# Hash-bit rows of pairs hashed alone, and the place of loads and output weights, in a fused attention and feed-forward kernel

## The chip, the cores and the metric

The kernel runs on one core of one Trainium2 chip. A core has a matrix engine (TensorE, PE in the profile), a vector engine (VectorE, DVE), an activation engine (ScalarE, ACT), a general engine (GpSimd, POOL) and SyncE (SP), which here only issues transfers. Each engine takes its own instructions in the order in which they were written, and waits on semaphores for what other engines and transfers have done. 16 DMA engines carry the transfers. The metric is the device time of one execution in microseconds; the median of several is compared.

## The reference, cut to what matters

Attention over 4 batches, 8 heads, 768 tokens and 64 dimensions. Six random projections give each token a bucket; a query sees only the keys of its own bucket. Behind it stands a gated feed-forward layer over all 3072 tokens.

```python
q_bits = np.einsum('bhsd,dk->bhsk', q, proj) > 0      # 6 bits; k_bits likewise
mask   = q_bucket[:, :, :, None] == k_bucket[:, :, None, :]
scores = np.where(mask, q @ k.T / sqrt(64), -1e9)
attn   = exp(scores - max) / (sum + 1e-9)
x      = (attn @ v) as 3072 x 512
xn     = x / sqrt(mean(x * x) + 1e-6) * rms_g
out    = (silu(xn @ w_gate) * (xn @ w_val)) @ w_out    # 512 -> 1536 -> 512
```

## The kernel before

**The mask is part of the product.** A head's q and k lie transposed in a tile `QK`, rows 0 to 63 the dimensions, rows 64 to 75 twelve rows made from the hash bits. For k a bit gives -32 or 0 and for q 16 or 0, in two rows for each bit, so that a key with another bit lowers the score so far that its exponential vanishes. One matmul over 76 rows (`KROWS`) gives the masked scores (`scores`, L344).

**The unit of work is a pair of heads**, written (batch, pair), as in (1,2). For a pair, q, k and v are loaded (`load_blocks`, L122, in four transfers of 96 KB for q or k with runs of 32 numbers; `load_rows`, L112, for v and for batch 0), turned (`turn_dve`, L194, VectorE, four steps each for k and q; `turn_pe` for batch 0 and pair (1,0)), cast into `QK` (`cast_pool`, L202, GpSimd), hashed, and v is cast and summed by GpSimd (`v_prep` L310, `v_sum` L316 to L318). The loads share ten buffers in turn.

**Hashing**: four products of the projection with k and q into one bank (`hash_bank`, L210), VectorE's comparison, which gives a tile of bits (`signs`, L217), and then the rows are moved to partitions 64 and up of `QK`. The pairs (1,1), (1,2) and (1,3) are hashed alone (`hash_lone`): one bank holds, for each half of the tokens, 32 rows for k and 32 for q, in which 12 rows are of the first head and the next 12 of the second. Eight transfers on SyncE's queue (L285) move 12 rows by 384 each. Pair (1,0) takes eight transfers of L268; batches 2 and 3 are hashed by two pairs at once (`hash_pairs`, L303).

**The order is written out by hand.** The loop runs over 192 slots of attention (a slot is a third of a head of one query half) and 48 more for what trails. `plan[s]` holds what is issued at slot s beside the scores and the exponential (`probs`, L354); `at(s, f, ...)` puts a step there, `rank` orders the steps within a slot. Nothing is moved by a scheduler: a step at a later slot stands behind all earlier steps in its engine's queue. Each transfer on SyncE's queue also waits for the eighth one before it. From slot 42 on, the feed-forward layer of query half w runs beside the attention of the halves after it, over 24 slots for each w: `gate` (L446), `value` (L456) with VectorE's L457 and L458 between, then `project` (L469), which needs the output weights `wo`, `ft` 0 to 5 from the first half's transfer and 6 to 11 from the second's. The hash products and the feed-forward products take turns in three banks of one pool (`gps`).

**Weights** come on GpSimd's own queue, cast on the way (`load_w` L520, `load_wo` L526): `wg` and `wv` in halves at slots 2, 6, 12 and 21, the two halves of `wo` at 43 and 50.

For a pair of `work`, `in_row(loads, s, hash_slot)` gives the slots of the k, q and v loads, the first slot of the eight turning steps, and the slot of the hash; the casts come at s + 4 and s + 8, v at s + 9. The first scores of (1,0) belong to slot 48, those of (1,1) to 60, of (1,2) to 66, of (1,3) to 72.

Of the kernel before, what the change touches and what calls it, by code (L numbers as in the profile page):

```python
# [8 lines left out]
FP32 = mybir.dt.float32  # L9
# [7 lines left out]
S = 768  # L17
D = 64
# [3 lines left out]
HALF = 384  # L22
KROWS = D + 12
# [17 lines left out]
BY_PE = [(0, hp) for hp in range(4)] + [(1, 0)]  # L41
# [3 lines left out]
def kernel(  # L45
# [12 lines left out]
    nc = tc.nc  # L58
    PSUM = bass.MemoryType.PSUM

    const = ctx.enter_context(tc.tile_pool(name="const", bufs=1))
# [20 lines left out]
    thr = const.tile([128, 1], FP32, name="thr")  # L82
    scl = const.tile([128, 1], FP32, name="scl")
    mhalf = const.tile([128, 3], FP32, name="mhalf")
    gcol = const.tile([128, 4], FP32, name="gcol")
    wg = const.tile([128, 4, DFF], FP16, name="wg")
    wv = const.tile([128, 4, DFF], FP16, name="wv")
# [39 lines left out]
    T0, QK = {}, {}  # L127
# [10 lines left out]
    def t0(b, h, which):  # L138
        hp, hh = divmod(h, 2)
        return T0[b, hp, which][:, hh * HALF : (hh + 1) * HALF]  # L140

    def k_cols(b, h, jt):
        o = (jt // 3) * S + (jt % 3) * 128 if (b, h // 2) in BY_PE else S + jt * 128
        return QK[b, h // 2][0:KROWS, h % 2, o : o + 128]

    def q_cols(w, h):
        b, half = divmod(w, 2)
        t = QK[b, h // 2][0:KROWS, h % 2]
        if (b, h // 2) in BY_PE:
            return t[:, half * S + HALF : (half + 1) * S]  # L150
        if b == 1:
            return t[:, 0:S].rearrange("p (c e t) -> p e c t", e=2, t=128)[:, half]
        return t[:, half * HALF : (half + 1) * HALF]
# [53 lines left out]
    def hash_bank(parts):  # L207
        ps = bank("d_ps", [128, HALF])
        for t, (w, src) in enumerate(parts):
            nc.tensor.matmul(  # L210
                ps[32 * t : 32 * t + 32, :], w, src,
                start=True, stop=True, tile_position=(0, 32 * t),
            )
        return ps

    def signs(bt, ps):
        nc.vector.tensor_scalar(  # L217
            out=bt, in0=ps, scalar1=thr, scalar2=scl, op0=ALU.is_gt, op1=ALU.mult
        )
# [6 lines left out]
    def bits_tile(i):  # L226

        if i % 2 == 0:
            held.append(spool.tile([128, S], FP16, name="bits", bufs=3))
        return held[-1][:, (i % 2) * HALF : (i % 2 + 1) * HALF]  # L230
# [43 lines left out]
    def hash_lone(b, hp):  # L274

        ps = hash_bank(
            [(w[:, 0:32], T0[b, hp, which][:, half * HALF : (half + 1) * HALF])
             for half in range(2) for w, which in ((pk, "k"), (pq, "q"))]
        )
        bt = bits_tile(0)  # L280
        signs(bt, ps)
        for hh in range(2):
            for half, j in ((0, 0), (0, 1), (1, 1), (1, 0)):
                p0, o = 64 * half + 32 * j + 12 * hh, (S, 0)[j] + half * HALF
                nc.sync.dma_start(  # L285
                    out=QK[b, hp][D:KROWS, hh, o : o + HALF], in_=bt[p0 : p0 + 12]
                )

    def hash_pairs(b, hps):
# [49 lines left out]
    def scores(g):  # L339
        w, h, p = SLOTS[g]  # L340
        ps = scps.tile([128, 2, 512], FP32, name="s_ps")
        idle(ps[:, 0, HALF:512], {0: 8, 3: 6}.get(g, 0))
        for j in range(2):
            nc.tensor.matmul(  # L344
                ps[:, j, 0:HALF], k_cols(w // 2, h, 2 * p + j), q_cols(w, h),
                start=True, stop=True,
            )
        sps[g] = ps
# [227 lines left out]
    def at(s, f, *a, rank=3):  # L576
        plan[s].append((rank, len(plan[s]), lambda: f(*a)))
# [36 lines left out]
    for i, (t, src) in enumerate(((wg, moe_w_gate), (wv, moe_w_val))):  # L614
        at(2 + 4 * i, load_w, t, src, 0, 768)
        at(12 + 9 * i, load_w, t, src, 768, 1536)
        at(43 + 7 * i, load_wo, 6 * i, 6 * i + 6)


    for which, sl in zip("kqv", (9, 11, 15)):  # L620
        at(sl, load_rows, nc.sync, 1, 0, which)
# [11 lines left out]
    def in_row(loads, s, hash_slot=None):  # L633
        return loads, range(s, s + 8), (s + 4, s + 8, s + 9), hash_slot

    work = {
        (1, 1): in_row((21, 32, 33), 42, 51), (1, 2): in_row((38, 42, 44), 49, 58),
        (1, 3): in_row((46, 52, 54), 56, 65),
        (2, 0): in_row((56, 60, 62), 64), (2, 1): in_row((63, 66, 69), 72, 81),
        (2, 2): in_row((71, 75, 78), 81), (2, 3): in_row((80, 83, 86), 89, 98),  # L640
        (3, 0): in_row((90, 94, 98), 100), (3, 1): in_row((100, 104, 108), 110, 119),
        (3, 2): in_row((116, 120, 124), 126), (3, 3): in_row((126, 130, 134), 136, 145),
    }
    for (b, hp), (loads, turns, cast_slots, sh) in work.items():
        for which, s in zip("kqv", loads):
            at(s, load_rows if which == "v" else load_blocks, nc.sync, b, hp, which)
        for i, s in enumerate(turns):
            at(s, turn_dve, b, hp, "kq"[i // 4], i % 4, rank=5)
        for which, s in zip("kq", cast_slots):
            at(s, cast_pool, b, hp, which)  # L650
        if sh:
            if b == 1:
                at(sh, hash_lone, b, hp)
            else:
                at(sh, hash_pairs, b, (hp - 1, hp))
        at(cast_slots[2], v_prep, b, hp)
        at(cast_slots[2], v_sum, b, hp)
        if b > 1 and hp % 2:
            at(48 * b + (17 if hp == 3 else -4), v_mean, b, hp - 1, 4)
# [18 lines left out]
    for w in range(8):  # L678
# [21 lines left out]
        for i in range(9 if w < 7 else 6):  # L700
            c, j = divmod(i, 3)
# [62 lines left out]
```

## Time and profile before

| | |
|---|---|
| median of 3 runs | 341.2 us (340.05 to 343.66) |
| profiled execution | 340.95 us, its span 339.2 us |
| mean granted clock of TensorE | 0.995 |
| busy in the span | PE 96%, DVE 70%, ACT 61%, POOL 46% |
| SyncE's transfers, share of the 16 DMA engines | 33.4%, in 82000 packets |
| weights on GpSimd's queue, share | 8.8%, in 3712 packets |
| transfers of bits by `hash_lone` | 24, issued from 69.1 to 104.0 us |

A page of the profile tells one execution. A row of a timeline gives the start, the length, the engine, the line, the operation and its operands; in square brackets stands how long the engine was idle before, and what ended that. A row of waits gives who waited for whom, with the total, the number of times and the longest. A window gives the busy time of each engine in a stretch, the clock that TensorE was granted as a share of full speed, the mean busy share of the DMA engines and what they moved. The ends of matmuls are modelled, so neighbours overlap a little. SPq and POOLq are the queues that issue transfers; their rows tell the issue, not the landing.

### The profile page before, as it was taken

Reading aid. Unit: us, or ns where it says so; the run is one execution under the profiler, and the core shown is the slowest. Engines: PE = TensorE matmul, PEld = TensorE weight load, DVE = VectorE, ACT = ScalarE, POOL = GpSimd, SP = SyncE. Lnnn points to the kernel's source line nnn. Section 1 sums busy time; section 2 is a strip of 40 time slices with the busy share of each in tenths; the row PEclk is TensorE's granted clock in tenths of the full one; section 3 lists DMA queues with packets and bytes.
Section 4 is the critical chain, followed back from the end, with each engine's and each line's share of the span. In section 5 each row is a group of like instructions: output and inputs, shape, how many; then the busy total and the mean of one; then the engine's idle time right before and its main releaser. Section 6 shows DMA issues by size and latency. Waiting matters only on the chain.

```text
span 339.2 us, 7797 instructions
## 1 busy us (share of the span) xinstructions
PE 326.1 (96%) x2983; PEld 200.2 (59%) x2983; DVE 237.7 (70%) x532; ACT 207.9 (61%) x324; POOL 155.6 (46%) x230
## 2 busy tenths in 40 slices
PE   8999989599989999999999999999999999999995
PEld 7566666265555655656565655656566655655653
DVE  4789669489587986978767794977356754784860
ACT  3789987356465755666665766666666766532321
POOL 4888766178745586374826156463101311130000
PEclk9999999989999999999999999999999999999999
DMA  7998929947273947605531572000110001001002
GB/s 236 334 231 192 140 50 183 175 79 135 44 177 78 199 56 178 109 9 119 124 82 24 109 121 90 22 12 7 38 56 2 3 31 64 2 1 62 33 0 93
DMA packets 85972, 31.36 MB, mean 92 GB/s; under 512 B 71480, under 2 KB 82992, under 8 KB 85936
## 3 DMA queue, kind: packets, MB, share of 16 engines
q1 hardware_dynamic: 82000, 26.09, 33.4%
q0 software_dynamic: 3712, 4.72, 8.8%
q8 instruction: 23, 0.38, 0.5%
q14 instruction: 13, 0.11, 0.1%
q10 hardware_dynamic: 224, 0.07, 0.1%
HBM read 28.32 MB, written 6.29 MB: 102 GB/s over the span
## 4 chain that ended last, share of the span: by engine, by line
PE 80%; DVE 8%; POOL 3%; DMA 3%; SPq 2%; issue 2%; ACT 1%; DVEq 0%; ACTq 0%; POOLq 0%
PE y_ps L469 18%; PE v_ps L456 16%; PE s_ps L344 14%; PE g_ps L446 13%; PE o_ps L366 8%; PE d_ps L210 4%; PE s_ps L446 3%; DMA kL<-in_k_dram 2%; PE x_ps L431 1%; SPq L122 1%; SPq L285 1%; PE z_ps L337 1%; PE t_ps L170 1%; DMA QK<-bits 1%; DVE t L457 1%
## 5 line engine op out<-in xcount | busy, mean ns | idle before, releaser
L354 ACT ACTIVATE psb<-s_ps 128x768 f16<-128x768 f32 x192 | 150.6, 809 | 33.5 <-PE s_ps L344 31.7
L344 PE MATMUL s_ps<-QK 76*128 76x384 f16 x384 | 93.7, 326 | 3.0 <-DMA QK<-bits 1.3
L456 PE MATMUL v_ps<-xnT,wv 128*128 128x384 f16 x384 | 78.7, 327 | 0.0
L469 PE MATMUL y_ps<-wo,ht 128*128 128x512 f16 x276 | 69.2, 379 | 0.1
L448 ACT ACTIVATE t<-g_ps 128x384 f32<-128x384 f32 x78 | 38.2, 490 | 48.0 <-PE g_ps L446 47.5
L457 DVE SCALAR_TENSOR_TENSOR t<-t,g_ps 128x384 f32<-128x384 f32 x78 | 42.7, 547 | 32.5 <-ACT t L448 32.1
L366 PEld LDWEIGHTS <-psb 128*128 128x128 f16 x1152 | 52.4, 98 | 22.0 <-issue 3.9
L446 PE MATMUL g_ps<-xnT,wg 128*128 128x384 f16 x312 | 63.5, 325 | 1.2 <-DVE xnT L432 0.6
L390 POOL TENSOR_TENSOR x<-otmp,rcp 128x384 f32<-128x384 f32 x31 | 25.9, 835 | 83.6 <-DVE rcp L386 83.1
L458 DVE SCALAR_TENSOR_TENSOR ht<-t,v_ps 128x384 f16<-128x384 f32 x96 | 53.2, 554 | 10.8 <-PE v_ps L456 1.5
L366 PE MATMUL o_ps<-vl,psb 128*128 128x65 f16 x1152 | 56.9, 194 | 0.0
L446 PEld LDWEIGHTS <-wg 128*128 128x128 f16 x384 | 36.1, 97 | 25.2 <-issue 1.7
L456 PEld LDWEIGHTS <-wv 128*128 128x128 f16 x384 | 36.4, 98 | 23.8 <-issue 0.9
L344 PEld LDWEIGHTS <-QK 76*128 76x128 f16 x384 | 31.3, 98 | 20.8 <-issue 8.2
L469 PEld LDWEIGHTS <-ht 128*128 128x128 f16 x276 | 25.9, 97 | 25.1 <-issue 1.5
L476 ACT COPY ysb<-y_ps 128x512 f32<-128x512 f32 x23 | 13.5, 586 | 25.3 <-PE y_ps L469 24.9
L402 POOL TENSOR_TENSOR sq<-x 128x384 f32<-128x384 f32 x31 | 25.7, 827 | 2.5
L432 DVE TENSOR_TENSOR xnT<-x_ps,gcol 128x512 f16<-128x512 f16 x24 | 16.2, 681 | 14.5 <-PE x_ps L431 14.5
L202 POOL CAST QK<-qT 64x768 f16<-64x768 f32 x22 | 18.2, 827 | 17.2 <-DVE qT L194 16.5
L194 DVE STREAM_TRANSPOSE kT<-kL 128x192 f32<-128x192 f32 x44 | 22.1, 516 | 4.3 <-issue 4.3
L381 DVE TENSOR_TENSOR otmp<-o_ps,cvb 128x390 f32<-128x390 f32 x32 | 17.9, 558 | 8.1 <-PE o_ps L366 8.0
L202 POOL CAST QK<-kT 64x768 f16<-64x768 f32 x22 | 18.2, 828 | 10.5 <-PE v_ps L456 4.1
(80 smaller groups left out, 301.7 us busy)
## 6 DMA issues: line engine op xcount, KB each, us to landing
vL<-in_v_dram SPq DMA_DIRECT2D x16, 384.0 KB
out_dram<-ysb SPq DMA_DIRECT2D x23, 256.0 KB
kL<-in_k_dram SPq DMA_DIRECT2D x44, 96.0 KB
qL<-in_q_dram SPq DMA_DIRECT2D x44, 96.0 KB
kL<-in_k_dram SPq DMA_DIRECT2D x4, 384.0 KB
qL<-in_q_dram SPq DMA_DIRECT2D x4, 384.0 KB
wg<-in_moe_w_gate_dram POOLq DMA_DIRECT2D x2, 768.0 KB, 7.2
wv<-in_moe_w_val_dram POOLq DMA_DIRECT2D x2, 768.0 KB, 8.4
```

The costliest lines, as they stand in the source:

```text
L202: nc.gpsimd.tensor_copy(QK[b, hp][0:64, hh, o : o + S], T0[b, hp, which][64 * hh : 64 * hh + 64, :])
L344: nc.tensor.matmul(ps[:, j, 0:HALF], k_cols(w // 2, h, 2 * p + j), q_cols(w, h), start=True, stop=True,)
L354: nc.scalar.activation(psb[w, h][:, p], sps.pop(g)[:, :, 0:HALF], AF.Exp, scale=ESCALE,)
L366: nc.tensor.matmul(o[:, c, hh, 0:65], psb[w, h][:, jt // 2, jt % 2, 128 * c : 128 * c + 128], vls[b % 2][:, h, v_chunk(b, h, jt), 0:65], s ...
L390: eng.tensor_mul(xd.rearrange("p c (h d) -> p c h d", h=2), tmp[:, :, :, 0:64], r.to_broadcast([128, 3, 2, 64]),)
L402: nc.gpsimd.tensor_mul(sq, xd, xd)
L446: nc.tensor.matmul(g, wg[:, kt, fs], xnT[w][:, kt], start=(kt == 0), stop=(kt == 3))
L448: nc.scalar.activation(t, g, AF.Tanh, scale=0.5)
L456: nc.tensor.matmul(vv, wv[:, kt, fs], xnT[w][:, kt], start=(kt == 0), stop=(kt == 3))
L457: nc.vector.scalar_tensor_tensor(out=t, in0=t, scalar=1.0, in1=g, op0=ALU.add, op1=ALU.mult)
L458: nc.vector.scalar_tensor_tensor(out=ht[w][:, ft], in0=t, scalar=0.5, in1=vv, op0=ALU.mult, op1=ALU.mult)
L469: nc.tensor.matmul(y, ht[w][:, ft, c * 128 : (c + 1) * 128], wo[:, ft, :], start=(ft == 0), stop=(ft == NF - 1),)
```

## The change

For pairs hashed alone `QK` keeps 24 rows of bits, and the scores' product runs over 88 rows. k's 24 rows (both heads' twelve) go to both heads' halves of the tile by one transfer for each half of the tokens, whose source is read twice: two transfers on SyncE's queue for a pair. q's 24 rows are written by GpSimd, multiplied row by row by a column of `own`, which is 1 on the rows of the head in question and 0 on the other's; four products of 24 by 384 for a pair. The zero rows of q take the other head's bits of k out of the sum. `own` is set at slot 45 by seven memsets.

The k, q and v loads of (1,1), (1,2) and (1,3) move to earlier slots, those of batch 2 by 2 to 4 slots. The halves of the output weights move from slots 43 and 50 to 31 and 52.

```diff
@@
+    own = const.tile([128, 2], FP32, name="own")
@@
+    def rows_of(b, hp):
+
+        return D + 24 if b == 1 and (b, hp) not in BY_PE else KROWS
+
     def k_cols(b, h, jt):
         o = (jt // 3) * S + (jt % 3) * 128 if (b, h // 2) in BY_PE else S + jt * 128
-        return QK[b, h // 2][0:KROWS, h % 2, o : o + 128]
+        return QK[b, h // 2][0 : rows_of(b, h // 2), h % 2, o : o + 128]
 
     def q_cols(w, h):
         b, half = divmod(w, 2)
-        t = QK[b, h // 2][0:KROWS, h % 2]
+        t = QK[b, h // 2][0 : rows_of(b, h // 2), h % 2]
@@
         bt = bits_tile(0)
         signs(bt, ps)
-        for hh in range(2):
-            for half, j in ((0, 0), (0, 1), (1, 1), (1, 0)):
-                p0, o = 64 * half + 32 * j + 12 * hh, (S, 0)[j] + half * HALF
-                nc.sync.dma_start(
-                    out=QK[b, hp][D:KROWS, hh, o : o + HALF], in_=bt[p0 : p0 + 12]
+        for half in range(2):
+            kb, qb = 64 * half, 64 * half + 32
+            nc.sync.dma_start(
+                out=QK[b, hp][D : D + 24, :, S + half * HALF : S + (half + 1) * HALF],
+                in_=bt[kb : kb + 24].unsqueeze(1).to_broadcast([24, 2, HALF]),
+            )
+            for hh in range(2):
+                nc.gpsimd.tensor_scalar_mul(
+                    QK[b, hp][D : D + 24, hh, half * HALF : (half + 1) * HALF],
+                    bt[qb : qb + 24], own[qb : qb + 24, hh : hh + 1],
                 )
@@
-        at(43 + 7 * i, load_wo, 6 * i, 6 * i + 6)
-
+        at(31 + 21 * i, load_wo, 6 * i, 6 * i + 6)
+
+    def rows_of_heads():
+
+        nc.gpsimd.memset(own, 0.0)
+        for p0 in (32, 96):
+            nc.gpsimd.memset(own[p0 : p0 + 24, 1:2], 1.0)
+            nc.gpsimd.memset(own[p0 : p0 + 12, 1:2], 0.0)
+            nc.gpsimd.memset(own[p0 : p0 + 12, 0:1], 1.0)
+
+    at(45, rows_of_heads)
@@
-        (1, 1): in_row((21, 32, 33), 42, 51), (1, 2): in_row((38, 42, 44), 49, 58),
-        (1, 3): in_row((46, 52, 54), 56, 65),
-        (2, 0): in_row((56, 60, 62), 64), (2, 1): in_row((63, 66, 69), 72, 81),
-        (2, 2): in_row((71, 75, 78), 81), (2, 3): in_row((80, 83, 86), 89, 98),
+        (1, 1): in_row((21, 22, 32), 42, 51), (1, 2): in_row((32, 33, 37), 49, 58),
+        (1, 3): in_row((38, 40, 44), 56, 65),
+        (2, 0): in_row((53, 55, 58), 64), (2, 1): in_row((59, 62, 66), 72, 81),
+        (2, 2): in_row((68, 71, 75), 81), (2, 3): in_row((78, 82, 86), 89, 98),
```

## The prediction

> **What bounds the kernel now.** First the page's head, then TensorE's own waits.
>
> ```profile
> span 339.2 us, 7797 instructions
> PE 326.1 (96%) x2983; PEld 200.2 (59%) x2983; DVE 237.7 (70%) x532; ACT 207.9 (61%) x324; POOL 155.6 (46%) x230
> ```
>
> TensorE (PE) is busy for 96% of the span; all its idle time is 13.1 us. An edit that leaves its matmuls alone can win only from that, and from stretches at a lower clock. Who ends its waits, as total, times and longest in us:
>
> ```profile
> PE d_ps L210 <- DVE t L457: 3.5, 1, 3.5
> PE s_ps L344 <- DMA QK<-bits: 1.3, 2, 1.1
> ```
>
> So two places matter: one wait for VectorE (DVE) at a hash product, two for bits that come by DMA. TensorE's timeline places them, with the products I use below:
>
> ```profile
> 55.87 0.49 PE L344 MATMUL s_ps<-QK 76*128 76x384 f16 x2
> 62.44 0.81 PE L446 MATMUL g_ps<-xnT,wg 128*128 128x384 f16 x4
> 66.73 0.56 PE L210 MATMUL d_ps<-kT,pk 128*32 128x384 f32 x1 [3.48 <-DVE t L457]
> 70.30 0.89 PE L446 MATMUL g_ps<-xnT,wg 128*128 128x384 f16 x4
> 80.40 0.49 PE L344 MATMUL s_ps<-QK 76*128 76x384 f16 x2
> 80.72 1.03 PE L469 MATMUL y_ps<-wo,ht 128*128 128x512 f16 x4
> 102.23 0.49 PE L344 MATMUL s_ps<-QK 76*128 76x384 f16 x2 [1.07 <-DMA QK<-bits]
> 106.77 0.48 PE L344 MATMUL s_ps<-QK 76*128 76x384 f16 x2 [0.23 <-DMA QK<-bits]
> ```
>
> The product at 66.73 is pair (1,1)'s hash (slot 51). The first wait costs more than its length, as the windows show (span, busy time of PE, PEld, DVE, ACT, POOL; then granted clock, DMA share, GB/s):
>
> ```profile
> 66.00:68.00 2.00, 1.27 (x9) 0.26 (x10) 1.86 (x6) 0.00 (x0) 0.00 (x0) 0.76 0.83 194
> 68.00:70.00 2.00, 2.00 (x10) 0.98 (x10) 1.69 (x5) 0.81 (x1) 1.74 (x3) 0.50 1.18 211
> 70.00:72.00 2.00, 2.00 (x19) 1.31 (x17) 1.24 (x3) 0.77 (x2) 1.92 (x3) 0.88 0.37 57
> 102.00:104.00 2.00, 1.77 (x19) 1.20 (x20) 0.84 (x3) 0.60 (x2) 1.11 (x2) 1.00 0.10 21
> ```
>
> After the 3.48 us gap the granted clock falls; the loss is 2 x (0.24 + 0.50 + 0.12) = 1.72 us. After the 1.07 us gap it stays 1.00.
>
> Behind the 3.48 us stands a load. The chain of waits (start, length, what):
>
> ```profile
> 55.60 5.84 DMA kL<-in_k_dram
> 61.44 4.33 issue
> ```
>
> VectorE's next instruction is the transpose of pair (1,2)'s k (slot 49). It has nothing else to wait for, and starts at 61.44 + 4.33 = 65.77; everything on VectorE queues behind it, the pass that frees the bank of the hash product too. Why the load is late, by SyncE's queue (SPq):
>
> ```profile
> 40.68 6.17 SPq L268 DMA_DIRECT2D QK<-bits  x8
> 50.45 8.08 SPq L122 DMA_DIRECT2D kL<-in_k_dram  x4
> 98.56 7.09 SPq L285 DMA_DIRECT2D QK<-bits  x8
> ```
>
> And by packets, MB and share of the DMA engines, from 61 to 62 us and then from 65 to 66 (q0 carries the weights, q1 SyncE's transfers):
>
> ```profile
> q0 software_dynamic: 165, 0.17, 104.3%
> q1 hardware_dynamic: 167, 0.02, 26.6%
> ```
>
> ```profile
> q1 hardware_dynamic: 1401, 0.18, 116.3%
> ```
>
> While output weights are moving, the 128-byte packets of the k loads get one turn for each weight packet, 167 in a microsecond; alone they get 1401. (1,2)'s k loads were issued from 50.45 on, into both halves of the output weights.
>
> **The change, part by part.** *Loads forward, output weights from slot 43 to 31.* q of (1,1) now stands ahead of the eight bit transfers of 40.68, so these end a few us later than 46.9, near 50, and (1,2)'s k is issued at about the old time. The bits' cover is the time to (1,0)'s first scores, 55.87; past that each us would be on the path. The first half of the weights is through by 50, and the second not yet asked for: four k transfers are 3072 packets, 2 to 3 us at the free rate, and I let them land by 55 to 57. Needed: 61.4. The stall goes. Removed: TensorE's pitch to the next instruction is 0.16 less than the modelled end of 63.25, so 3.48 + 0.16 = **3.64 us**, and **1.72 us** of clock.
>
> What is late next: VectorE.
>
> ```profile
> 68.28 0.60 DVE L217 TENSOR_SCALAR bits<-d_ps,thr,scl 128x384 f16<-128x384 f32 x1
> 69.15 0.54 DVE L457 SCALAR_TENSOR_TENSOR t<-t,g_ps 128x384 f32<-128x384 f32 x1
> ```
>
> The pass at 69.15 ends 3.92 us after the transpose at 65.77. With that transpose right behind the one before, at 61.45, it ends at 65.37. TensorE, with its hash product at 63.09 and at full clock, would want the bank for the g_ps of 70.30 at about 65.1 (that is 3.57 after the product, less some 1.5 of the slow clock). A new wait of **0.25 us**. So TensorE is ahead by 3.64 + 1.72 - 0.25 = 5.1 us from here.
>
> The first weights' issue comes to stand ahead of the norm on GpSimd (POOL), and the seven memsets of `own` ahead of (1,1)'s casts:
>
> ```profile
> 43.54 0.19 POOL L415 TENSOR_SCALAR ms<-ss 128x3 f32<-128x3 f32 x1 [2.56 <-DVE ss L413]
> 57.72 0.89 POOL L526 DMA_DIRECT2D wo<-in_moe_w_out_dram  x1
> 61.51 1.70 POOL L202 CAST QK<-qT 64x768 f16<-64x768 f32 x2 [2.90 <-DVE qT L194]
> 68.19 0.82 POOL L390 TENSOR_TENSOR x<-otmp,rcp 128x384 f32<-128x384 f32 x1 [4.98 <-DVE rcp L386]
> ```
>
> The issue (0.9 us) fits into the idle 2.56 us before 43.54, so it costs nothing; without that gap it would delay the norm and the first g_ps by up to 0.9. Seven memsets are at most seven of the small copies costed below, 3.5 us; the second weights' issue (0.89) leaves that place, and the 2.90 us takes the rest.
>
> *Bits of lone pairs.* Eight transfers on SyncE's queue (7.09 us at 98.56) become two, and four GpSimd products of 24x384 come in per pair. The 88 rows of the scores cost TensorE nothing that I can name: the moving columns stay 384. With two transfers, and (1,3)'s and batch 2's loads earlier, SyncE no longer runs behind when pair (1,3)'s bits are made. The waits of 1.07 and 0.23 go: **1.30 us**. The products have no row; by rows of GpSimd (busy us, mean ns):
>
> ```profile
> L316 POOL TENSOR_TENSOR vadd<-vL 128x384 f32<-128x384 f32 x12 | 12.1, 1011 | 0.0
> L415 POOL TENSOR_SCALAR ms<-ss 128x3 f32<-128x3 f32 x8 | 1.6, 195 | 25.3 <-DVE ss L413 25.2
> L250 POOL COPY QK<-bits 12x384 f16<-12x384 f16 x1 | 0.5, 500 | 0.8 <-DVE bits L217 0.8
> ```
>
> One product costs between 0.195 and 1.011; I take the copy's 0.50, of the same type and row length, so 2.0 per pair.
>
> *What they queue before.* GpSimd is in order, and the second half of the output weights (slot 50 before, 52 now) comes to stand behind (1,1)'s products and behind its v cast and sums:
>
> ```profile
> 69.86 0.82 POOL L310 CAST vl<-vL 128x768 f16<-128x768 f32 x1
> 72.64 1.70 POOL L202 CAST QK<-kT 64x768 f16<-64x768 f32 x2
> 89.08 1.70 POOL L202 CAST QK<-qT 64x768 f16<-64x768 f32 x2
> ```
>
> The x product (68.19) comes 2.42 after VectorE's 65.77, so now at 63.87; it and its square take 69.86 - 68.19 = 1.67, to 65.54. The bits are ready before: 68.28 + 0.60 is 3.11 after 65.77, so 64.56. Products to 67.54; v cast and sums, 72.64 - 69.86 = 2.78, to 70.32; there the weights are issued, 12.6 us later than at 57.72. From issue to landing (last number, us), the second half, the first half, and a gate load:
>
> ```profile
> wo<-in_moe_w_out_dram POOLq DMA_DIRECT2D x1, 768.0 KB, 7.6
> ```
>
> ```profile
> wo<-in_moe_w_out_dram POOLq DMA_DIRECT2D x1, 768.0 KB, 9.6
> ```
>
> ```profile
> wg<-in_moe_w_gate_dram POOLq DMA_DIRECT2D x1, 768.0 KB, 7.1
> ```
>
> I take 7.6, the same half's own: landing at 77.9. It is needed by the third product of the y_ps group of 80.72 (slot 59, `ft` 6), about 0.6 after its start, less 5.1: 76.2. A new wait of **1.7 us**, on the path, since all of TensorE's queue stands behind it.
>
> Other waiters: the scores of (1,1), 80.40 - 5.1 = 75.3, want products done at 67.5: no wait. For (1,3) even the worst case, all of GpSimd's added 4.9 us undigested on top of 89.08 + 1.70, and 2.0 for its own products, ends at 97.7; its scores come at 102.23 - 1.07 - 3.4 = 97.8. Loads of batches 2 and 3 are needed where TensorE has no wait today, and come a few slots earlier: nothing.
>
> **Sum**, against the profiled execution's 340.95 us (0.25 below the runs' median of 341.2): -3.64 - 1.72 + 0.25 - 1.30 + 1.7 = -4.7, so **336.2 us**; without the new weight wait 334.5.
>
> The trace leaves open from which gap the clock falls: 1.07 us idle left it at 1.00, 3.48 us halved it. 1.7 lies nearer to the first, and I count no loss; if it does fall, the time is 336.2 + 1.72 = 337.9. The Trainium skill, "TensorE: Matmul & The Clock Gate", HAM oscillation, wants gaps above about 3.4 us for that; both rows agree with it, and by it the 337.9 does not come.
>
> A rule that speaks against the change: the Trainium skill, "SBUF — State Buffer", Who interferes with whom, has GpSimd and VectorE lock each other out of a shared port for whole instructions, and blames late weight transfers of this queue on it. By it the products and the landing move to their upper ends, which is the slower rival below.
>
> **Rivals.** (1) *The weights come in time.* Products at 0.195 and landing in 7.1 give 70.32 - 1.22 + 7.1 = 76.2: no wait, **334.5 us**. For it: the gate load's 7.1. Against: the products move a full row of 384, as the copy does.
> (2) *The weights come so late that the clock falls.* With 9.6 the wait is 3.7 and the clock's 1.72 come back: 334.5 + 5.4 = **339.9 us**. For it: the 9.6 is the same transfer's other half, among loads; now q of (2,0) is still moving when it starts.
> (3) *Slower: GpSimd becomes the bound of slot 59.* Products at 1.011 as well: issue at 72.4, landing at 82.0, a wait of 5.8 and the clock, 334.5 + 7.5 = **342.0 us**. It decides from a landing at 80.9 on, where 4.7 of wait plus 1.72 eat all that was won. Against: the casts at 72.64, of rows twice as long, take 0.85 each.
> (4) *The stall stays*, because (1,2)'s k is still late: SyncE issues it only after q of (1,1) and the bits of 40.68. Then only the 1.30 goes: **339.7 us**. It needs a landing after 61.4, 5 us past my estimate.
>
> **How the numbers follow.** Forecast 0.45, rival 1 0.20, rival 2 0.16, rival 3 0.09, rival 4 0.06; 0.04 for anything slower that I don't see. Range 333.7 to 340.4: from just below rival 1 (0.25 of VectorE's wait, and run to run scatter) to above 2 and 4; rival 3 and the rest stay out. Of this kernel's time a measurement can tell about 1% from no change: below 337.8 is faster, above 344.6 slower. Faster: the forecast and rival 1, less the forecast's few cases above 337.8 (the clock), 0.63. Slower by over 1%: the unseen 0.04 and part of rival 3, 0.08. Within: 0.29.
>
> **What would show it.** Right: no wait for VectorE at the hash product, granted clock 1.00 from 60 to 72; SPq with two transfers a pair; no wait for QK<-bits at 97; a new gap of 1 to 3 us in a y_ps group near 76, ended by wo. Products near 0.5 us. Wrong: a VectorE transpose still idle for its load; clock below 1.00 after the y_ps gap; GpSimd's products near 1 us; or a new wait ahead of 55, where (1,0)'s bits now queue behind one more load.

## The result, and the profile after

The changed kernel takes 342.62 us (median of 20 runs, 341.36 to 344.46), the kernel before 340.55 (20 runs): ratio 1.0061, 95% interval 1.0043 to 1.0080. It is 0.6% slower, where 336.2 was forecast and 340.4 was the upper end of the range. The profiled execution took 342.25 us, 1.3 more than the 340.95 of before. Of the kernels measured further on, the ratios leave out two slow executions: the profiled one of old_bits, at 674.95 us, and one of only_bits, at 346.23 us.

The head of the page for the changed kernel:

```profile
span 340.4 us, 7789 instructions
PE 326.2 (96%) x2983; PEld 200.2 (59%) x2983; DVE 238.1 (70%) x532; ACT 207.9 (61%) x324; POOL 171.0 (50%) x249
```

TensorE's busy time is that of before; GpSimd's is 15.4 us longer. TensorE's own waits (total, times, longest):

```profile
PE y_ps L479 <- DMA wo<-in_moe_w_out_dram: 6.2, 1, 6.2
```

Both waits of before, the one for VectorE at the hash product and the two for bits, are gone from this list, and one wait for the second half of the output weights has come. TensorE's timeline around it:

```profile
63.48 0.51 PE L215 MATMUL d_ps<-kT,pk 128*32 128x384 f32 x1
...
75.86 0.60 PE L479 MATMUL y_ps<-wo,ht 128*128 128x512 f16 x2
82.65 1.01 PE L479 MATMUL y_ps<-wo,ht 128*128 128x512 f16 x2 [6.20 <-DMA wo<-in_moe_w_out_dram]
```

The hash product of pair (1,1) starts at 63.48 with no gap before it (66.73 and 3.48 idle in before). The y_ps group that stood at 80.72 now starts at 75.86, and stops after two of its four products for 6.20 us. The windows (span, busy time of PE, PEld, DVE, ACT, POOL; granted clock, DMA share, GB/s):

```profile
66.00:68.00 2.00, 2.00 (x22) 1.33 (x20) 1.89 (x4) 1.20 (x2) 1.83 (x2) 1.00 0.87 242
...
80.00:82.00 2.00, 0.00 (x0) 0.00 (x0) 1.58 (x4) 0.00 (x0) 1.84 (x3) 0.51 1.13 266
82.00:84.00 2.00, 1.35 (x12) 0.79 (x12) 0.00 (x0) 0.00 (x0) 1.93 (x2) 0.50 1.43 181
84.00:86.00 2.00, 2.00 (x9) 0.84 (x7) 0.00 (x0) 0.81 (x1) 1.82 (x3) 0.50 0.60 71
86.00:88.00 2.00, 2.00 (x12) 0.95 (x11) 0.66 (x2) 1.38 (x2) 1.94 (x3) 0.78 0.00 0
```

The clock holds at the old place (66 to 68, where it stood at 0.76 before) and falls behind the new gap: from 82.65 on it costs 1.35 x 0.50 + 2 x 0.50 + 2 x 0.22 = 2.1 us. So the place of the loss has moved, and it has grown from 3.48 + 1.72 to 6.20 + 2.1.

Why the weights are late stands in GpSimd's timeline:

```profile
64.27 0.83 POOL L400 TENSOR_TENSOR x<-otmp,rcp 128x384 f32<-128x384 f32 x1 [0.77 <-DVE rcp L396]
65.17 0.83 POOL L412 TENSOR_TENSOR sq<-x 128x384 f32<-128x384 f32 x1
66.10 5.20 POOL L294 TENSOR_SCALAR QK<-bits,own 24x384 f16<-24x384 f16 x4
71.37 0.82 POOL L320 CAST vl<-vL 128x768 f16<-128x768 f32 x1
...
74.17 0.94 POOL L536 DMA_DIRECT2D wo<-in_moe_w_out_dram  x1
```

Four products take 5.20 us, not 2.0; the issue comes at 74.17, not 70.32. The chain of waits takes it from there to the product at 82.65 (start, length, what):

```profile
74.17 8.43 DMA wo<-in_moe_w_out_dram
```

And the price of one product, by groups (busy us, mean ns):

```profile
L294 POOL TENSOR_SCALAR QK<-bits,own 24x384 f16<-24x384 f16 x12 | 14.9, 1240 | 1.0
```

1240 ns for one, not the 500 of the copy, and above the upper bound of 1011 ns that the prediction gave. SyncE's queue did what was forecast: the four transfers of (1,2)'s k at once, and two transfers of bits for a lone pair.

```profile
42.14 8.18 SPq L273 DMA_DIRECT2D QK<-bits  x8
...
50.98 2.85 SPq L123 DMA_DIRECT2D kL<-in_k_dram  x4
...
65.65 1.77 SPq L289 DMA_DIRECT2D QK<-bits  x2
```

### The profile page after: what moved, and what is told of

It reads as the page before. It is cut to its first block, busy times and chain, and to the rows that moved or that the text cites. A ratio compares the mean times of both kernels' runs of the same rounds, so it can differ in the third digit from the quotient of the medians.

```text
span 340.4 us, 7789 instructions
## 1 busy us (share of the span) xinstructions
PE 326.2 (96%) x2983; PEld 200.2 (59%) x2983; DVE 238.1 (70%) x532; ACT 207.9 (61%) x324; POOL 171.0 (50%) x249
## 4 chain that ended last, share of the span: by engine, by line
PE 81%; DVE 7%; POOL 5%; DMA 3%; ACT 1%; issue 1%; SPq 0%; DVEq 0%; POOLq 0%; ACTq 0%
PE y_ps L479 18%; PE v_ps L466 16%; PE s_ps L354 14%; PE g_ps L456 14%; PE o_ps L376 8%; PE s_ps L456 3%; PE d_ps L215 3%; DMA wo<-in_moe_w_out_dram 2%; POOL QK L294 1%; PE x_ps L441 1%; PE t_ps L175 1%; PE z_ps L347 1%; POOL QK L191 1%; PE y_ps L740 1%; DMA qL<-in_q_dram 1%
## 5 line engine op out<-in xcount | busy, mean ns | idle before, releaser
L354 PE MATMUL s_ps<-QK 76*128 76x384 f16 (+1 forms) x384 | 94.3, 327 | 1.9 <-ACT psb L364 1.2
L479 PE MATMUL y_ps<-wo,ht 128*128 128x512 f16 x276 | 70.7, 384 | 6.2 <-DMA wo<-in_moe_w_out_dram 6.2
L354 PEld LDWEIGHTS <-QK 76*128 76x128 f16 (+1 forms) x384 | 31.6, 98 | 19.5 <-issue 6.5
```

What stands on the lines that cost most here:

```text
L354: nc.tensor.matmul(ps[:, j, 0:HALF], k_cols(w // 2, h, 2 * p + j), q_cols(w, h), start=True, stop=True,)
L479: nc.tensor.matmul(y, ht[w][:, ft, c * 128 : (c + 1) * 128], wo[:, ft, :], start=(ft == 0), stop=(ft == NF - 1),)
```

## The experiments

The theory from this profile: the loads and the weights' early first half do save the 5.4 us of the old stall; what eats them is the product's price, by way of the issue that queues behind four of them. Rivals: the weights' slot 52 is wrong whatever the products cost; or GpSimd is too full with the products wherever the weights stand. The parts were taken one by one:

| kernel | loads of batches 1 and 2 | weights in slots | lone bits | median us | ratio to before (95%) |
|---|---|---|---|---|---|
| only_wo | old | 31, 52 | old | 338.82 | 0.9947 (0.9924 to 0.9969) |
| old_bits_old_wo | forward | 43, 50 | old | 341.18 | 1.0007 (0.9987 to 1.0027) |
| old_bits | forward | 31, 52 | old | 335.72 | 0.9834 (0.9802 to 0.9866) |
| old_bits_again (the same) | forward | 31, 52 | old | 335.47 | 0.9840 (0.9796 to 0.9884) |
| old_bits_wo50 | forward | 31, 50 | old | 340.04 | 0.9969 (0.9943 to 0.9995) |
| only_bits | old | 43, 50 | product, column | 341.03 | 1.0001 (0.9973 to 1.0029) |
| the change | forward | 31, 52 | product, column | 342.62 | 1.0061 (1.0043 to 1.0080) |
| wo2_50 | forward | 31, 50 | product, column | 340.55 | 0.9978 (0.9960 to 0.9995) |
| copies | forward | 31, 52 | copy | 337.43 | 0.9879 (0.9841 to 0.9917) |
| tensors_wo52 | forward | 31, 52 | product, two tensors | 340.37 | 0.9986 (0.9957 to 1.0015) |
| tensors_wo50 | forward | 31, 50 | product, two tensors | 334.44 | 0.9810 (0.9763 to 0.9858) |

### The second half of the weights in slot 50

```diff
-        at(31 + 21 * i, load_wo, 6 * i, 6 * i + 6)
+        at(31 + 19 * i, load_wo, 6 * i, 6 * i + 6)
```

> The changed kernel with the second half of the output weights back at slot 50, ahead of GpSimd's products. Theory A (the loss is the wait of 6.2 us for these weights and about 2.1 us of slow clock behind it, and nothing else): both go, 342.6 - 8.3 = about 334.3 us. Theory B (the products at 1.24 us each also fill GpSimd: in the changed kernel it is busy without a gap from 64 to 100 us): TensorE, now 8.3 us earlier, waits for the rows of (1,2) about 1.8 us and for those of (1,3) about 1.2 us more, 337.3 us. Either way no wait for wo at slot 59.

340.55 us: the wait for the weights is gone, the time is not, and neither of the two expected times came. GpSimd's timeline, then VectorE's, then TensorE's, in this kernel:

```profile
94.19 5.22 POOL L294 TENSOR_SCALAR QK<-bits,own 24x384 f16<-24x384 f16 x4
...
104.97 0.83 POOL L412 TENSOR_TENSOR sq<-x 128x384 f32<-128x384 f32 x1
```

```profile
105.83 0.55 DVE L416 TENSOR_REDUCE ssp<-sq 128x3 f32<-128x384 f32 x1 [4.25 <-POOL sq L412]
```

```profile
106.90 1.44 PE L466 MATMUL v_ps<-xnT,wv 128*128 128x384 f16 x4 [3.20 <-DVE t L467]
```

The four products of the third pair put off the squares, VectorE stands 4.25 us for them, and TensorE 3.20 us for VectorE. A window of ten microseconds (columns as above) shows GpSimd full, at 9.34 of 10, and the clock falling there too:

```profile
100.00:110.00 10.00, 6.80 (x48) 3.81 (x46) 5.33 (x13) 3.59 (x6) 9.34 (x14) 0.84 0.50 93
```

So the place of the weights is only one of two ways in which the products cost time. With the weights out of the way the same 15 us of GpSimd work come out some 25 us later, at the squares, a waiter that the prediction did not list.

### The old bits with the new loads and weights

```diff
-        for half in range(2):
-            kb, qb = 64 * half, 64 * half + 32
...
+        for hh in range(2):
+            for half, j in ((0, 0), (0, 1), (1, 1), (1, 0)):
+                p0, o = 64 * half + 32 * j + 12 * hh, (S, 0)[j] + half * HALF
+                nc.sync.dma_start(
+                    out=QK[b, hp][D:KROWS, hh, o : o + HALF], in_=bt[p0 : p0 + 12]
                 )
```

> The changed kernel with the bits of lone pairs moved as before (eight transfers of 12 rows, 76 rows in the scores, no products, no own); loads and output weights as changed (31 and 52). If the products are what made the weights late: the issue of the second half comes 5.3 us earlier, at about 68.9, landing at about 77.3, a wait of about 1.2 us at slot 59 in place of 6.2, no slow clock, 342.6 - 8.3 + 1.2 = 335.5 us. If the slot alone (52, behind the v sums) made them late: a wait above 4 us remains, above 339. If SyncE falls behind again with 24 transfers: waits for bits near 97 us, 1 to 2 us more.

> The kernel of old_bits once more, for its profile and with the runs of its neighbours: bits moved by eight transfers, loads and output weights as changed (31 and 52). The products made the weights late: the issue of the second half near 69, a wait for wo at slot 59 of about 1.2 us, granted clock 1.00 behind it; 335.7 us as measured. The slot alone made them late: a wait above 4 us and a lower clock. SyncE behind: waits for QK<-bits near 97.

335.72 and 335.47 us. Without its new bits the change is worth 1.6%. In the second of the two GpSimd issues the weights 6.1 us earlier than in the changed kernel, by its timeline:

```profile
68.03 0.94 POOL L531 DMA_DIRECT2D wo<-in_moe_w_out_dram  x1
```

They land 7.7 us after this issue, and TensorE does not wait for them at all (1.2 us had been expected); what is left is one wait for bits on SyncE's fuller queue, by TensorE's timeline:

```profile
97.03 0.48 PE L349 MATMUL s_ps<-QK 76*128 76x384 f16 x2 [1.29 <-DMA QK<-bits]
```

The new bits thus save 1.3 us at most here, and cost about 7 us net (342.62 - 335.47).

### Copies in place of the products

```diff
-                nc.gpsimd.tensor_scalar_mul(
+                nc.gpsimd.tensor_copy(
                     QK[b, hp][D : D + 24, hh, half * HALF : (half + 1) * HALF],
-                    bt[qb : qb + 24], own[qb : qb + 24, hh : hh + 1],
+                    bt[qb : qb + 24],
                 )
```

> The changed kernel with a plain GpSimd copy of the same 24x384 in place of each product; it leaves out the selection by head, so q's bits of both heads stand in both heads' rows. It tests the prediction's sum at its own price of 0.50 us: issue of the weights at about 71.0, landing after 8.4 at 79.4, a wait of about 3.2 us. If the clock falls only after 3.4 us of idling: 342.6 - 8.3 + 3.2 = 337.5 us. If it falls earlier: 339.6 us.

337.43 us. Groups by form, TensorE's timeline and the windows:

```profile
L294 POOL COPY QK<-bits 24x384 f16<-24x384 f16 x12 | 5.8, 511 | 1.0 <-DVE bits L222 0.8
```

```profile
80.00 0.59 PE L479 MATMUL y_ps<-wo,ht 128*128 128x512 f16 x2 [2.89 <-DMA wo<-in_moe_w_out_dram]
```

```profile
60.00:70.00 10.00, 10.00 (x95) 5.93 (x94) 9.22 (x22) 6.32 (x11) 6.48 (x10) 1.00 0.89 167
...
80.00:90.00 10.00, 10.00 (x94) 5.59 (x94) 5.02 (x11) 5.84 (x8) 8.69 (x13) 1.00 0.89 164
```

This is the changed kernel at the price that the prediction took, without the selection by head. It is 1.2 us above the forecast. The wait for the weights is 2.9 us instead of 1.7, and the clock holds behind it. The clock of this execution falls at another place, though, long before the first copy at 66.72:

```profile
30.00:40.00 10.00, 9.74 (x113) 7.38 (x109) 5.88 (x13) 7.85 (x12) 7.18 (x11) 0.83 0.93 169
```

That is 10 x 0.17 = 1.7 us, where the kernel before and the changed kernel hold 1.00. No term of the sum stands for it, and what brought it is open. One of the four executions of this kernel kept a mean granted clock of 1.000, and took 335.76 us. So with a product at 0.50 us the kernel comes within about a microsecond of the forecast, though not term by term; it is the price of the product that does not hold.

### What makes the product dear

One kernel, with a copy for pair (1,1), a product with a constant for (1,2) and a product of two tensors for (1,3):

```diff
+                if hp == 1:
+                    nc.gpsimd.tensor_copy(dst, src)
+                elif hp == 2:
+                    nc.gpsimd.tensor_scalar_mul(dst, src, 1.0)
+                else:
+                    nc.gpsimd.tensor_mul(
+                        dst, src, own[qb : qb + 24, hh : hh + 1].to_broadcast([24, HALF])
+                    )
```

> One look at the price of the product. Pair (1,1) with four plain copies, (1,2) with four products by the constant 1.0 (both leave out the selection by head), (1,3) with four products of two tensors, the column of own read along the row with step 0 (the selection is kept). If the column operand makes the price: copy 0.50, constant 0.50, two tensors about 0.8. If the operation itself does, whatever its scalar: copy 0.50, constant 1.24, two tensors 0.8 or more. If 24 partitions or 16-bit reading do: all three near 1.24.

336.03 us in a single run. Groups by form:

```profile
L299 POOL TENSOR_SCALAR QK<-bits 24x384 f16<-24x384 f16 x4 | 4.7, 1180 | 0.3
L301 POOL TENSOR_TENSOR QK<-bits,own 24x384 f16<-24x384 f16 x4 | 3.2, 821 | 0.2
L297 POOL COPY QK<-bits 24x384 f16<-24x384 f16 x4 | 1.9, 500 | 0.1
```

Partitions, columns, type and the tiles are the same in the three rows, so it is the operation: a product of a tensor with a number takes 1180 ns even where the number is a constant, 60 less than with a column of `own`, and a product of two tensors, which does the same work on one operand more, only 821. It isn't the neighbourhood either: all twelve copies have a mean of 511 in the places where all twelve products have 1240. This also answers the rule that the prediction set against the change. The Trainium skill, "SBUF — State Buffer", Who interferes with whom, has GpSimd and VectorE lock each other out of a shared port; no such lengthening shows in the copies (a mean of 511 ns over all three places, the first of them in a stretch with VectorE busy for 9.22 of 10 us, against 500 for the single copy in the kernel before), which speaks against the lock as what made the products long.

### The cheaper product, in both slots

```diff
-                nc.gpsimd.tensor_scalar_mul(
+                nc.gpsimd.tensor_mul(
                     QK[b, hp][D : D + 24, hh, half * HALF : (half + 1) * HALF],
-                    bt[qb : qb + 24], own[qb : qb + 24, hh : hh + 1],
+                    bt[qb : qb + 24],
+                    own[qb : qb + 24, hh : hh + 1].to_broadcast([24, HALF]),
                 )
```

The first of the two kernels also has the weights' second half in slot 50, the second leaves it in slot 52.

> wo2_50 with the products as a product of two tensors (0.82 us each in the look at prices, in place of 1.24), the selection kept: 1.7 us less on GpSimd for each pair, 5 in all up to the squares that VectorE waited 4.25 us for in wo2_50. If GpSimd's fill is what cost wo2_50 its gain: the wait of 3.2 us and its slow clock (1.7) go, 340.6 - 5 = about 335.5 us. If it is something else (the second input, the port): about 340.5 as wo2_50.

> The changed kernel with GpSimd's product of two tensors (821 ns measured at this shape) in place of the product with a column (1240 ns), output weights in slots 31 and 52 as in the change. Four products before the issue of the second half take 4 x 0.42 = 1.7 us less, so the issue goes from 74.2 to about 72.5 and the wait for it from 6.2 to about 4.4 us; that is over the 3.2 us after which the granted clock fell elsewhere, so about 2 us more follow it: 342.6 - 1.8 = 340.8, less what GpSimd's fuller queue cost later (up to 0.5). If the wait came out under 2.9 us and the clock held, 337 to 338. If GpSimd's fill rather than the place of the second half were what costs the changed kernel its time, it would be near the 334.4 us that the same products gave with the second half in slot 50.

334.44 us with slot 50, the fastest kernel of this study, 1.9% under the kernel before. The windows:

```profile
90.00:100.00 10.00, 9.51 (x89) 6.05 (x88) 9.24 (x21) 7.05 (x12) 9.41 (x13) 1.00 0.90 184
100.00:110.00 10.00, 10.00 (x100) 6.56 (x99) 8.81 (x22) 6.68 (x12) 7.91 (x11) 1.00 0.42 83
```

TensorE waits for neither the weights nor the squares. GpSimd is busy for 9.4 of 10 us here too, but it has nearly caught up when the squares are wanted: VectorE waits 0.46 us for them, where it waited 4.25 in wo2_50, and from 100 to 110 GpSimd is busy for 7.91 of 10, against 9.34.

340.37 us with slot 52, as expected. GpSimd's timeline, TensorE's, and a window:

```profile
71.97 0.94 POOL L537 DMA_DIRECT2D wo<-in_moe_w_out_dram  x1
```

```profile
80.23 0.67 PE L480 MATMUL y_ps<-wo,ht 128*128 128x512 f16 x2 [4.02 <-DMA wo<-in_moe_w_out_dram]
```

```profile
80.00:90.00 10.00, 9.77 (x78) 5.47 (x78) 3.89 (x9) 5.07 (x7) 8.94 (x13) 0.83 0.86 166
```

4.02 us of wait, with the clock at 0.83 in the ten microseconds behind it (10 x 0.17 = 1.7 us): that is 5.7 us, where the medians of the two kernels differ by 5.9 and their profiled executions (339.45 and 334.26) by 5.2. So a cheap product alone does not do, nor does the earlier slot alone (340.55); both together do.

### Slot 50 with the old bits

The old bits as above, and slot 50 in place of 52.

> old_bits with the second half of the output weights at slot 50 in place of 52: issued near 58.6 us, ahead of the v sums. If old_bits' remaining wait is for these weights: it goes, 335.7 - 1.2 = 334.5 us. If the weights, now moving from 60 to 65 beside the loads of (1,3), make those late for VectorE at about 73: a wait of VectorE for a load and no gain, 335.7 us or more.

340.04 us, with runs spread from 337.76 to 341.94. In the profiled execution, at 341.67 one of the slowest, the stall of the kernel before is back. TensorE's wait, then SyncE's queue, GpSimd's issue of the second half, and VectorE's transpose:

```profile
PE d_ps L215 <- DVE t L462: 3.9, 1, 3.9
```

```profile
46.44 8.39 SPq L273 DMA_DIRECT2D QK<-bits  x8
...
55.50 4.54 SPq L123 DMA_DIRECT2D kL<-in_k_dram  x4
```

```profile
57.70 0.94 POOL L531 DMA_DIRECT2D wo<-in_moe_w_out_dram  x1
```

```profile
66.23 0.52 DVE L199 STREAM_TRANSPOSE kT<-kL 128x192 f32<-128x192 f32 x1 [4.78 <-DMA kL<-in_k_dram]
```

The last of the k transfers goes out at 60.04, after the weights at 57.70, and lands only for 66.2. In this execution SyncE ran 4.3 us later than in the changed kernel by the time of the bits (46.44 against 42.14); why, among the same loads, stays open.

### The new bits alone

```diff
-        for hh in range(2):
-            for half, j in ((0, 0), (0, 1), (1, 1), (1, 0)):
...
+            for hh in range(2):
+                nc.gpsimd.tensor_scalar_mul(
```

This is the kernel before with the new bits and `own`, all loads and weights at their old slots.

> The kernel before with the new bits alone (24 rows, two transfers, four products, own); loads and output weights where they were (43 and 50, ahead of the products). The stall for (1,2)'s k and its slow clock stay (5.2 us), the weights are in time. If the products cost nothing where the weights stand ahead of them: the waits for bits (1.3) go, 341.0 - 1.3 = 339.7 us. If they fill GpSimd: 15 us more between 66 and 108, where it was busy 29 of 42 before; VectorE waits for GpSimd's squares near 105, 1 to 3 us, 341 to 343 us.

341.03 us, no change. In the profiled execution (341.15) the waits for bits are gone, and so, against what was expected, is the stall for (1,2)'s k with its clock: 1.3 and 5.2 us. GpSimd's queue took as much, mostly at the place that wo2_50 showed, in the waits below and in a clock of 0.83 from 100 to 110 us (1.7 us). So the new bits cost some 7 us here too, and that the time lies in the expected range is luck. TensorE's waits:

```profile
PE v_ps L466 <- DVE t L467: 3.6, 2, 3.2
PE g_ps L456 <- DVE t L467: 1.5, 2, 1.0
...
PE s_ps L354 <- POOL QK L294: 0.9, 2, 0.6
```

Around the stall that is missing, SyncE's queue and GpSimd's issue stand so:

```profile
50.65 7.17 SPq L123 DMA_DIRECT2D kL<-in_k_dram  x4
```

```profile
57.90 0.89 POOL L536 DMA_DIRECT2D wo<-in_moe_w_out_dram  x1
```

The last k transfer goes out at 57.82, just ahead of the weights. In the kernel before it went out at 58.53, behind an issue at 57.72. This made a theory: the stall comes where k's last transfer goes out after the second half of the weights. Two more kernels tested it.

### The weights' slots alone, and the loads alone

Edits: in the kernel before only `at(43 + 7 * i, ...)` to `at(31 + 21 * i, ...)`; then only the loads of batches 1 and 2.

> The kernel before with the two halves of the output weights in slots 31 and 52, and nothing else of the change: batch 1's loads stay where they were, the lone pairs keep eight transfers of 12 rows. Theory A: TensorE's stall at pair (1,1)'s hash product appears where SyncE's last transfer for (1,2)'s k goes out after GpSimd has issued the second half of the output weights. It does in the kernel before (50.45 + 8.08 = 58.53 against 57.72) and with the old bits and the second half in slot 50 (55.50 + 4.54 = 60.04 against 57.70), and does not where the stall is missing: the kernel after, the old bits with slots 31 and 52 (53.8 against 68.0), the new bits alone (57.82 against 57.90). Here the k would be issued by about 56 and the second half at about 66, so no stall: 340.95 - 3.64 - 1.72 = 335.6, with the waits for bits at QK kept, and up to 1.2 for the second half: 335.6 to 336.8. Theory B: the loads have to be forward as well, since the k has to be issued before about 54; then the stall stays and the time is 339.7 to 341.

> The kernel before with batch 1's loads forward and nothing else of the change: output weights in slots 43 and 50, eight transfers of 12 rows. Theory A (the stall comes where the last transfer for (1,2)'s k goes out after the second half of the output weights): the first half goes out at about 49 and moves until about 57, beside the k, whose four transfers then take 7 to 8 us from about 49.5; their end lies within 1 us of the second half's issue at about 57.8, so this kernel stands at the edge: 335.5 where it ends before, 339.7 or more where it ends after, and the profile's two numbers say which of them belongs to the profiled execution. Theory B (loads forward alone take the stall away): 335.5 whichever of the two comes first.

Weights alone: 338.82 us. The stall is gone (windows, TensorE full and the clock at 1.00), as theory A said; but the gain is 2.0 us instead of 5.4. TensorE, now ahead, runs into SyncE's queue. A window, TensorE's timeline and the sum of its waits for bits:

```profile
60.00:70.00 10.00, 10.00 (x95) 5.96 (x94) 9.14 (x21) 6.28 (x10) 7.08 (x10) 1.00 0.45 82
```

```profile
100.01 0.48 PE L344 MATMUL s_ps<-QK 76*128 76x384 f16 x2 [2.87 <-DMA QK<-bits]
```

```profile
PE s_ps L344 <- DMA QK<-bits: 3.4, 2, 2.9
```

That sum is 3.4 us, against 1.3 in the kernel before: 340.95 - 5.36 + 2.1 = 337.7, and the three executions with a mean granted clock of 1.000, the profiled one among them, took 337.55 to 338.34. The other seven had 0.988 to 0.995 and took 338.56 to 341.05; no trace shows where their clock fell.

Loads alone: 341.18 us, nothing gained. SyncE's queue and GpSimd's issue:

```profile
50.10 7.97 SPq L123 DMA_DIRECT2D kL<-in_k_dram  x4
```

```profile
57.73 0.89 POOL L531 DMA_DIRECT2D wo<-in_moe_w_out_dram  x1
```

Here k's last transfer goes out at 58.07, after the weights, so the theory as it was put asks for the stall; it did not come. The limit, if it is one of time, lies between 0.34 us (no stall) and 0.81 us (the kernel before) after the issue. The packets fit such a limit: from 59 to 60 us, when the weights begin to move (44 packets here, 41 in the kernel before), SyncE's transfers still moved 688 packets here and only 109 there. These are single executions, so the limit is argued and not shown. Theory B has the stall right in this kernel, but not the time; and the weights alone took the stall away with the loads where they were. What came in its place is two waits for the bits of (1,1) and (1,2), the second with a fall of the clock behind it (last section), which stand in SyncE's queue behind loads that move beside the weights. TensorE's timeline:

```profile
77.66 0.48 PE L349 MATMUL s_ps<-QK 76*128 76x384 f16 x2 [2.22 <-DMA QK<-bits]
89.18 0.48 PE L349 MATMUL s_ps<-QK 76*128 76x384 f16 x2 [2.60 <-DMA QK<-bits]
```

So neither the loads (0) nor the weights (-2.0) give much alone; together they give -5.5 (old_bits_again), because each takes away the wait on which the other's gain would be lost.

## Why the prediction was wrong, step by step

**The stall and its clock (-3.64, -1.72): right.** No wait at the hash product, clock 1.00 there. The y_ps group of 80.72 started at 75.86, 4.9 us earlier; the net lead was reckoned at 5.1. The kernel without the products, old_bits_again, has the whole of it: 335.5.

**VectorE late with a bank (+0.25): did not show.** No such wait is in the list.

**The waits for bits (-1.30): right for the changed kernel,** where none is left. The old bits still wait 1.29 us in its place.

**The casts, the memsets, the issue ahead of the norm at nothing: right,** as far as TensorE's list of waits shows nothing there.

**The products (0.50 each, bounds 0.195 to 1.011): the step that failed.** They took 1.24 us, 1.30 from one to the next. The bounds were rows of other work: a sum of two tensors of 128x384, and the one row of the same operation, with only 3 columns, in which the part that grows with the columns can't be seen. The copy between them was taken for its "same type and row length", and it is the operation that sets the price. Through the same queue this moved the issue by 5.20 - 2.0 = 3.2 us, to which 0.6 came from x, its square and the gaps between instructions: 74.17 instead of 70.32.

**The landing (7.6): 0.8 us too short.** It took 8.43; with the issue's 3.85 and the group's start 0.2 to 0.3 later than reckoned this makes 6.2 of wait instead of 1.7.

**The clock behind the new wait (0 counted): 2.1 us.** It came behind a wait of 6.2 us instead of 1.7. Rival 3 had this whole mechanism, with an issue at 72.4, a landing at 82.0, a wait of 5.8 and 342.0 us; a chance of 0.09 was too little for it, since its price, at the upper bound, was still below the true one. That its time comes so near is in part luck: its issue is 1.8 us too early, and its landing time of 9.6 is 1.2 too long.

The sum with the measured terms: -3.64 - 1.72 - 1.30 + 6.2 + 2.1 = +1.6, and +1.3 was measured between the two profiled executions.

**"For (1,3) even the worst case" (nothing): wrong in wo2_50 and only_bits.** That step asked when the scores want the products, and not who else stands in GpSimd's queue behind them. The squares of the norm do, and there the third pair's products cost 3.2 us and the clock. In the changed kernel GpSimd ends these squares no earlier (at 106.8 us, against 105.8 in wo2_50), but TensorE has stood 6.2 us for the weights and wants them later, so this second cost did not show in its trace.

## What to carry to other kernels

Price an operation that the trace does not show by a row of the same operation, and when the only such row is tiny, put the upper bound above every row of the same size, not at one of them; then ask what a full engine's whole queue releases, not only the result that the edit adds. An issue of a large transfer on a computing engine inherits every microsecond put ahead of it, so it belongs ahead of new work: with the cheap products the issue two slots earlier was worth 5.9 us. The earlier place has to be checked against the loads there: with the old bits the same two slots cost 4.6 us. And two edits that each move a wait may be worth little alone (0 and 2.0 us) and 5.5 us together, so parts of a change should be measured in pairs as well.

## What the runs showed of the hardware

On GpSimd a product of a 24x384 fp16 tensor with a column took 1240 ns, with a constant 1180, of two tensors 821, and a copy 500. That the product with one operand is the dearest was not expected.

The granted clock does not follow from the length of one gap of TensorE as the trace shows it. It fell after 3.2 us (only_bits and wo2_50), held after 2.87 and 2.89 (the profiled executions of only_wo and copies), and in old_bits_old_wo fell after 2.60, as its windows show (columns as above):

```profile
90.00:92.00 2.00, 2.00 (x12) 0.57 (x5) 1.72 (x3) 0.57 (x1) 0.86 (x2) 0.70 0.09 22
92.00:94.00 2.00, 2.00 (x14) 1.10 (x13) 0.00 (x0) 0.00 (x0) 0.00 (x0) 0.50 0.52 157
```

In copies it stood at 0.50 from 32 to 34 us, and the gaps of TensorE ahead of that fall were 0.50, 0.30 and 0.26 us long. The Trainium skill, "TensorE: Matmul & The Clock Gate", HAM oscillation, names gaps above about 3.4 us; four falls here come after shorter ones. What else decides was not tried.
